# Second MLP product of batches 1 to 7 by seven block products for a pair of token tiles, with memory laid out anew and values cast by their transfer

## The chip, the cores and the metric

The kernel runs on one core of a Trainium2 chip. The metric is the device time of one execution in microseconds (us). The engines are named as the profile names them: PE is TensorE (PEld its weight loads), DVE is VectorE, ACT is ScalarE, POOL is GpSimd and SP is SyncE, which issues transfers and transposes. A trailing q (SPq) is an engine's queue.

## The reference

Attention over 8 batches of 12 heads (448 tokens, 64 features a head), with q and k normalised per token, then a layer norm, a multilayer perceptron of 768 to 3072 to 768 with a relu, and the residual:

```python
q_n, k_n = rmsnorm(q, g_q), rmsnorm(k, g_k)
scores = q_n @ k_n.transpose(0, 1, 3, 2) / sqrt(64)
attn_out = softmax(scores) @ v                      # (8, 12, 448, 64)
x = attn_out.transpose(0, 2, 1, 3).reshape(8, 448, 768)
xn = (x - mean(x)) / sqrt(var(x) + 1e-6) * g_ln
out = x + maximum(xn @ w_ch1, 0.0) @ w_ch2          # 768 x 3072, 3072 x 768
```

All inputs and the output are float32.

## The kernel before

Heads are taken in pairs, six to a batch. A *unit* is one or, in the steady part, two pairs whose q, k and v are loaded and prepared together. Preparation is a list of one-letter pieces (prep_ops): `a` squares the keys on ACT into the tile khl, `c` squares the queries into qn (line L116), `d` and `e` sum the squares on DVE (ssq, L266), `g` turns sums into scales, `i` multiplies keys by the product of both gains on POOL (L274), `j` and `k` split a key into a high and a low fp16 half (khl; L108, L282), `l` and `m` make the fp16 queries (qn; L91, L319), `v` and `w` cast values to fp16 on POOL (v16, vl; L322, L328), `x` transposes the keys into kU and `y` the queries into qU by transfers of SP (L298 to L311). khl, qn and the load tile qkv have two buffers each; kU and qU have two as well.

Attention of a pair runs in seven *steps*: per step one score product (psS, L408) on PE, an exp on ACT (E, L440) and one value product of the pair before (oA, oB; L477, L479). Two PSUM banks named psS and the bank of tr take turns for scores. At a pair's end DVE divides (L490 to L497), writes the tokens' rows x (xl for the last 64 tokens of two batches, put together as a fourth tile), and takes statistics (L990).

Batch 0 is done in phases by token tiles, in an order written out by hand (the table ORDER). For batches 1 to 7 the MLP of batch b runs beside the attention of batch b + 1. mlp_chunks(b) yields *chunks*, each with a cost: 24 up chunks (six matmuls psH, L1056, and a relu on ACT into hT, L1058), and then, for every token tile and half of the 768 output columns, four down chunks of six matmuls of 384 columns (psC, L1090), the result of which DVE scales and adds to x (L1097). Odd batches have four tiles of 128 tokens (up products of 512 columns), even ones three (384 columns). run_rest emits the attention steps between chunks in proportion to cost, so that they end 13 chunks early:

```python
emit()
done += cost
upto(int(min(goal, start + (goal - start) * done / (total - 960 * tail))))   # tail = 13
if self.pos >= goal and items is None:
    items = self.ln_list(b + 1)
```

In those last 13 chunks the layer norm of batch b + 1 runs: the aggregate (L1005), the norm xn of each tile (L1010, on DVE), and its transpose into xnT by SP (L1038). The first up product of batch b + 1 needs all of xnT. Batch 7 has no attention beside it.

psH, psC and a few others share the three PSUM banks of the pool ps_m. PE, ACT, POOL and SP issue in the order of the code; the place of an instruction on DVE is chosen by a scheduler when the program is built, and is then fixed too.

## Time and profile before

| | |
|---|---|
| median of 3 runs | 592.93 us (591.63 to 593.49) |
| the profiled execution | 591.01 us, span 589.4 us |
| PE busy | 577.6 us, 98% of the span |
| ACT, DVE, POOL busy | 353.0, 291.7, 189.5 us |
| second products psC (L1090) | 1368 matmuls |
| up products psH (L1056) | 1008 matmuls |
| DMA | 75.25 MB, 128 GB/s over the span |

The span goes from the first to the last instruction; the execution's own time includes some 1.6 us around it. The busy time of an engine is the sum over its instructions without overlaps; matmuls are pipelined, so the mean of one (323 ns for psC) is longer than the interval between two.

### The profile page before, as it was taken

The numbers are of one execution on the slowest core, as the hardware profiler recorded it, in microseconds if no ns is written. First come the engines' busy times: TensorE is split into PE (matmuls) and PEld (weight loads), VectorE is DVE, ScalarE is ACT, GpSimd is POOL, SyncE is SP. The second block draws the span as 40 slices with busy tenths as digits, with TensorE's granted clock in tenths as the row PEclk, the third lists the DMA queues.
The fourth block names the chain that finished last, engine by engine and source line by source line (L and its number), as shares of the span: only waits on it lengthen the run. The fifth ranks groups of instructions, "written<-read, shape, count | busy, mean of one in ns | idle before, by whom it ended". The sixth has DMA issues, their size and how long they took to land.

```text
span 589.4 us, 12424 instructions
## 1 busy us (share of the span) xinstructions
PE 577.6 (98%) x4971; PEld 360.4 (61%) x4971; DVE 291.7 (49%) x636; ACT 353.0 (60%) x666; POOL 189.5 (32%) x258
## 2 busy tenths in 40 slices
PE   5899999999999999999999999999999999999997
PEld 5799976545666666545566666655566566654565
DVE  6999688345545456624446256815266222540011
ACT  5999773488752997178842797358844477124300
POOL 4648261065350665044350465342502000000000
PEclk9999999999999999999999999999999999999999
DMA  8999998573594987843779596844823220030011
GB/s 266 226 246 219 228 220 213 115 192 89 114 181 125 132 161 115 191 131 66 124 133 158 99 140 140 174 133 92 155 59 88 69 63 1 33 103 1 1 53 57
DMA packets 130321, 75.25 MB, mean 128 GB/s; under 512 B 96564, under 2 KB 120452, under 8 KB 130260
## 3 DMA queue, kind: packets, MB, share of 16 engines
q1 hardware_dynamic: 113712, 44.94, 37.3%
q0 software_dynamic: 16224, 29.27, 23.7%
q8 instruction: 40, 0.66, 0.5%
q10 hardware_dynamic: 324, 0.21, 0.1%
q14 instruction: 21, 0.17, 0.1%
HBM read 52.30 MB, written 11.01 MB: 107 GB/s over the span
## 4 chain that ended last, share of the span: by engine, by line
PE 95%; SPq 2%; DVE 1%; DMA 1%; ACT 0%; issue 0%
PE psC L1090 37%; PE psH L1056 33%; PE psS L408 8%; PE oA L477 5%; PE psU L749 4%; PE oB L479 2%; PE psS L426 2%; PE psS L693 1%; SPq L167 1%; SPq L175 1%; PE oA L725 1%; DMA qkv<-in_q_dram 1%; PE tr L345 1%; PE tr L362 0%; ACT E L704 0%; DVE khl L573 0%
## 5 line engine op out<-in xcount | busy, mean ns | idle before, releaser
L1090 PE MATMUL psC<-w,hT 128*128 128x384 f16 (+1 forms) x1368 | 235.6, 323 | 0.0
L1056 PE MATMUL psH<-xnT,w 128*128 128x512 f16 (+1 forms) x1008 | 217.3, 356 | 0.0
L440 ACT ACTIVATE E<-psS,rr_all 128x448 f16<-128x448 f32 x264 | 164.6, 636 | 58.3 <-PE psS L408 57.6
L1090 PEld LDWEIGHTS <-hT 128*128 128x128 f16 x1368 | 128.2, 98 | 75.9 <-issue 0.4
L1058 ACT ACTIVATE hT<-psH 128x512 f16<-128x512 f32 (+1 forms) x168 | 93.7, 558 | 112.3 <-PE psH L1056 110.8
L1056 PEld LDWEIGHTS <-w 128*128 128x128 f16 x1008 | 91.1, 98 | 77.0 <-issue 2.1
L408 PE MATMUL psS<-qU,kU 128*128 128x448 f16 x252 | 86.3, 352 | 0.0
L477 PEld LDWEIGHTS <-E 128*128 128x128 f16 x792 | 53.6, 98 | 34.4 <-issue 2.1
L1097 DVE SCALAR_TENSOR_TENSOR x<-psC,rs_all,x 128x384 f32<-128x384 f32 x48 | 29.0, 616 | 75.6 <-PE psC L1090 75.1
L274 POOL TENSOR_TENSOR qkv<-qkv,gprod 128x896 f32<-128x896 f32 x19 | 39.5, 2079 | 76.9 <-ACT khl L116 62.4
L477 PE MATMUL oA<-v,E 128*128 128x65 f16 x756 | 57.8, 193 | 0.1
L490 DVE RECIPROCAL rec_all<-oA 128x6 f32<-128x6 f32 x42 | 8.2, 195 | 88.6 <-PE oA L477 88.2
L167 POOL DMA_DIRECT2D qkv<-in_k_dram x14 | 11.1, 796 | 118.3 <-ACT E L440 53.4
L266 DVE TENSOR_REDUCE ssq<-khl 128x14 f32<-128x896 f32 x21 | 22.7, 1083 | 53.3 <-ACT khl L116 53.2
L479 PE MATMUL oB<-v,E 128*128 128x65 f16 x252 | 45.0, 193 | 0.1
L408 PEld LDWEIGHTS <-kU 128*128 128x128 f16 x252 | 24.3, 98 | 15.3
L266 DVE TENSOR_REDUCE ssq<-qn 128x14 f32<-128x896 f32 x21 | 22.8, 1084 | 21.1 <-ACT qn L116 21.1
L91 DVE SCALAR_TENSOR_TENSOR qn<-qkv,rr_all 128x256 f16<-128x256 f32 (+2 forms) x71 | 25.3, 416 | 15.1 <-ACT rr_all L270 15.1
L749 PE MATMUL psU<-xnT,w 128*128 128x128 f16 x432 | 27.0, 219 | 0.0
L749 PEld LDWEIGHTS <-w 128*128 128x128 f16 x432 | 25.2, 98 | 1.5 <-issue 0.4
L479 PEld LDWEIGHTS <-E 128*128 128x128 f16 x264 | 25.4, 96 | 0.3 <-DVE xl L497 0.2
L492 DVE TENSOR_TENSOR x<-oA,rec_all 128x384 f32<-128x384 f32 x42 | 23.4, 558 | 1.3
(161 smaller groups left out, 602.5 us busy)
## 6 DMA issues: line engine op xcount, KB each, us to landing
out_dram<-x SPq DMA_DIRECT2D x20, 384.0 KB, 2.6
qkv<-in_v_dram POOLq DMA_DIRECT2D x15, 384.0 KB, 6.6
qkv<-in_k_dram POOLq DMA_DIRECT2D x14, 384.0 KB, 4.0
qkv<-in_q_dram POOLq DMA_DIRECT2D x14, 384.0 KB, 4.9
w<-in_moe_w_ch_dram POOLq DMA_DIRECT2D x3, 1536.0 KB, 13.2
w<-in_moe_w_ch_dram POOLq DMA_DIRECT2D x8, 576.0 KB, 13.0
qkv<-in_q_dram SPq DMA_DIRECT2D x7, 384.0 KB, 8.0
qkv<-in_v_dram SPq DMA_DIRECT2D x6, 384.0 KB, 10.8
```

The costliest lines, as they stand in the source:

```text
L91: nc.vector.scalar_tensor_tensor(out=out, in0=x, scalar=8.0, in1=r.unsqueeze(2).broadcast_to([x.shape[0], g, D]), op0=ALU.mult, op1=ALU.mult)
L266: nc.vector.tensor_reduce(out=c["ssq"][:, n], in_=c["sq", n], axis=AX.X, op=ALU.add)
L274: _on(nc, f"i{u}", "P").tensor_tensor(out=self.loads[u][1], in0=self.loads[u][1], in1=sh.gprod.unsqueeze(1).broadcast_to([128, g, D]), op= ...
L408: self.nc.tensor.matmul(ps[:, 0:S], c["main"][:, ts(i, 128)], c["q"][:, ts(i // 3, S)], start=True, stop=True)
L440: self.nc.scalar.activation(out=o, in_=c.pop(("ps", i))[:, 0:S], func=AFT.Exp, scale=self.units[u][3][:, g:g + 1], bias=EXP_BIAS)
L477: nc.tensor.matmul(oA[:, t, cs], E[:, ts(t, 128)], rhs, start=(i == 0 and t == 0), stop=(i == 6 and t == 2))
L479: nc.tensor.matmul(oB[:, cs], E[:, 320:448], rhs, start=(i == 0), stop=(i == 6))
L749: nc.tensor.matmul(ps[:, ts(f, 128)], sh.w1[:, dc, ts(4 * k + f, 128)], self.xnT[:, dc, ts(t, 128)], start=(f == 0 and dc == 0), stop=(f = ...
L1056: nc.tensor.matmul(ps[:, 0:N], sh.w1[:, dc, ts(f, 128)], xnT[:, dc, 0:N], start=(dc == 0), stop=(dc == NDC - 1))
L1058: nc.scalar.activation(out=hT[:, f, 0:N], in_=ps[:, 0:N], func=AFT.Relu)
L1090: nc.tensor.matmul(self.psC[:, 0:g[1]], self.hT[:, f, ts(t, 128)], sh.w2[:, h, f, c:c + g[1]], start=(f == 0), stop=(f == NFF - 1))
L1097: self.nc.vector.scalar_tensor_tensor(out=x, in0=self.sums.pop((b, t, g[0]))[:, 0:g[1]], scalar=self.rs[:, b, t:t + 1], in1=x, op0=ALU.mul ...
```

## The change

For two neighbouring token tiles of one batch the second product is a 2 x 2 block product: two row blocks (the tiles a and a + 1) of two inner halves (the first 12 and the last 12 of the 24 chunks of hT, `lo` and `hi`) by two inner halves of two column halves of w2. It is now computed by seven products of blocks with 12 matmuls each, not eight, which needs sums of blocks beforehand and of results behind. In an odd batch two pairs of tiles are done so, in an even batch one pair, and its third tile as before in chunks named U, V and W. Batch 0 keeps the old way.

```diff
+        for f in range(NFF):
+            yield 6 * N / 2.4, (lambda f=f: (up(f), self.after_up(b, f)))
+        yield from self.products(b, n)
+
+    def after_up(self, b, f):
+        if b == 1 and f % 4 == 3:
+            self.weight_sums(f // 4)
+        if f in (11, 17):
+            self.sums_of(0, "3", slice(0, 6) if f == 11 else slice(6, 12), self.xn)
+        if f in (19, 23):
+            self.sums_of(0, "1", slice(0, 6) if f == 19 else slice(6, 12))
...
+    def sums_of(self, a, which, f, room=None):
...
+        if which == "3":
...
+            tt(out=o[:, f], in0=lo(a), in1=lo(a + 1), op=ALU.subtract)
+        elif which == "1":
+            tt(out=lo(a + 1), in0=lo(a + 1), in1=hi(a + 1), op=ALU.add)
+        elif which == "2":
+            tt(out=lo(a), in0=lo(a + 1), in1=lo(a), op=ALU.subtract)
+        else:
+            tt(out=hi(a), in0=hi(a), in1=lo(a), op=ALU.subtract)
...
+        def gather(p6, p7, a):
+            def call():
+                u = kept(a)
+                tt(out=u, in0=six(c[p6][:, 0:384]), in1=u, op=ALU.add)
+                self.free(c.pop(p6))
+                x = six(tiles[a][:, 384:DM])
+                stt(out=x, in0=u, scalar=self.rs[:, b, a:a + 1], in1=x, op0=ALU.mult, op1=ALU.add)
+                tt(out=u, in0=six(c[p7][:, 0:384]), in1=u, op=ALU.add)
+                self.free(c.pop(p7))
...
+            product(key(1), lo(a), wl(0), True, True, sums(a, "2"), keep(key(1), a), read(key(1), a, L))
+            product(key(7), third, wx(1), True, True)
+            product(key(6), lo(a), wx(0), True, True, gather(key(6), key(7), a))
+            product(key(2), hi(a), wh(0), True, True, sums(a, "4"), read(key(2), a, L), *behind,
+                    *([put(a, L)] if end else []))
+            product(key(5), lo(a + 1), wl(1), True, True, read(key(5), a, R, last=False), read(key(5), a + 1, R))
+            product(key(4), hi(a + 1), wx(2), True, True, read(key(4), a + 1, L), put(a + 1))
...
+                product(key(3), hi(a), wh(1), True, True, read(key(3), a, R), put(a, R if end else slice(0, DM)),
+                        *([flush] if a + 2 == n else []))
```

The four sums of a pair are single fp16 tensor_tensor instructions on DVE (L1150 to L1156), those of the first pair of a batch partly in halves after up chunks. Batch 1 also makes three sums of blocks of w2, once for all batches (weight_sums, 24 instructions). A result that is needed twice is kept on ACT (keep, L1209). The bank of each product is freed by its read (L1186, L1194) or by the gather (L1214 to L1223).

Room for the weight sums is found by a new layout. One tile `room` holds load tiles, E rows and weight sums in turn. From unit 9 (STEADY) there is one buffer for khl, one for qn, and one load tile for q and k; E has nine rows handed out one by one; xn has two buffers for batches 2 to 7 instead of four; the sums' scratch rt is single. The three banks of ps_m are handed out by a list written into the code. The values of units from 9 on are loaded straight into v16 and vl as fp16, by six transfers a unit issued by POOL, in place of a load and POOL's casts:

```diff
+        if u >= STEADY and n == 2:
+            s0 = UNIT_PAIR[u] % 6
+            out = self.v16[:, s0:s0 + m].rearrange("p s h j d -> p (s h) j d")
+            for h in range(2 * m):
+                self.nc.gpsimd.dma_start(out[:, h, :, 0:D], self.v[b, hs + h, 0:384].rearrange(
+                    "(p j) d -> p j d", j=3))
+            left = self.v[b, hs:hs + 2 * m, 384:448].rearrange("(w e) p d -> e p w d", e=2)
+            for e in range(2):
+                self.nc.gpsimd.dma_start(self.vl[64 * e:64 * e + 64, s0:s0 + m, e, 0:D], left[e])
+            return
...
-            c["khl"] = self.p_n.tile([128, 14, 2, D], FP16, tag="khl", name="khl")[:, 0:g]
+            c["khl"] = self.split_tile("khl", u >= STEADY)[:, 0:g]
...
-                c["qn"] = self.p_n.tile([128, 14, 2, D], FP16, tag="qn", name="qn")[:, 0:g]
+                c["qn"] = self.split_tile("qn", u >= STEADY)[:, 0:g]
...
+            s = 7 * (UNIT_PAIR[u] - 2)
+            for at, names in ((-6, "V"), (-8, "bai"), (-7, "d"), (-5, "jc"), (-4, "e"), (-3, "kg"), (-2, "lK"),
+                              (-1, "mQ"), (0, "x"), (1, "y")):
```

The last lines set at which attention step, relative to s, each piece of a unit is issued; a unit has 14 steps. K and Q stand for the loads of the next unit's keys and queries, V for the casting load of this unit's values.

The order on DVE at the end of batch 1 is shown next. BN_AGGR is the aggregate and xn the norms of batch 2; psC reads belong to batch 1. Before:

```order
L492 TENSOR_TENSOR x<-oA,rec_all 128x3x128
L497 TENSOR_TENSOR xl<-oB,rec_all 64x128
L990 BN_STATS stat<-x 128x6 x3
L1005 BN_AGGR stat<-stat 128x2 x3
L1010 SCALAR_TENSOR_TENSOR xn<-x,stat,gln 128x768 x3
L1097 SCALAR_TENSOR_TENSOR x<-psC,rs_all,x 128x384 x2
L282 TENSOR_TENSOR khl<-qkv,khl 128x14x64
```

After, at the same place:

```order
L546 TENSOR_TENSOR x<-oA,rec_all 128x3x128
L551 TENSOR_TENSOR xl<-oB,rec_all 64x128
L1045 BN_STATS stat<-x 128x6 x3
L1060 BN_AGGR stat<-stat 128x2 x3
L1065 SCALAR_TENSOR_TENSOR xn<-x,stat,gln 128x768 x2
L1154 TENSOR_TENSOR hT<-hT 128x12x128
L1186 SCALAR_TENSOR_TENSOR x<-psC,rs_all,x 128x384
L308 TENSOR_REDUCE ssq<-khl 128x14
L1065 SCALAR_TENSOR_TENSOR xn<-x,stat,gln 128x768
L1214 TENSOR_TENSOR hT<-psC,hT 128x6x64
```

The second sum of the second pair (L1154) and a read now stand behind two of the three norms, and the third norm behind them.

At the end of batch 2, on DVE, three norms and a fourth for xl stood ahead of the reads; before:

```order
L1005 BN_AGGR stat<-stat 128x2 x4
L1010 SCALAR_TENSOR_TENSOR xn<-x,stat,gln 128x768 x3
L1010 SCALAR_TENSOR_TENSOR xn<-xl,stat,gln 128x768
L1097 SCALAR_TENSOR_TENSOR x<-psC,rs_all,x 128x384 x2
L282 TENSOR_TENSOR khl<-qkv,khl 128x14x64
```

After:

```order
L1060 BN_AGGR stat<-stat 128x2 x4
L1065 SCALAR_TENSOR_TENSOR xn<-x,stat,gln 128x768 x2
L1186 SCALAR_TENSOR_TENSOR x<-psC,rs_all,x 128x384 x3
L1065 SCALAR_TENSOR_TENSOR xn<-x,stat,gln 128x768
L1065 SCALAR_TENSOR_TENSOR xn<-xl,stat,gln 128x768
L1186 SCALAR_TENSOR_TENSOR x<-psC,rs_all,x 128x384
L1194 SCALAR_TENSOR_TENSOR x<-psC,rs_all,x 128x768
```

Three reads (products 5, 5 and 4) have moved between the norms.

On ACT, in batch 2, around the squares of keys and queries (L116), with what each instruction waits for (DMAHW are the transposes and loads of SP, DMASW the loads of POOL); before:

```order
L116 ACTIVATE khl<-qkv 128x896 [waits DMAHW4_49,DMAHW5_49,DMASW7_49,DMAHW6_49,DMASW6_49,DMASW0_49]
L440 ACTIVATE E<-psS,rr_all 128x448 [waits PE_49]
L1058 ACTIVATE hT<-psH 128x384 [waits PE_49]
L440 ACTIVATE E<-psS,rr_all 128x448 [waits PE_49]
L116 ACTIVATE qn<-qkv 128x896 [waits DMAHW1_49,DMAHW2_49,DMAHW0_49,DMAHW3_49,DMASW3_49,DMAHW7_49,DMASW2_49,DMASW1_49]
L440 ACTIVATE E<-psS_5190,rr_all 128x448 [waits PE_49]
```

After:

```order
L116 ACTIVATE khl<-room 128x896 [waits DMAHW5_49,DMAHW6_49,DMASW7_49,DMAHW7_49,DMASW1_49,DMASW0_49]
L1113 ACTIVATE hT<-psH 128x384 [waits PE_49]
L492 ACTIVATE room<-psS,rr_all 128x448 [waits PE_49]
L1113 ACTIVATE hT<-psH 128x384 [waits PE_49]
L492 ACTIVATE room<-psS_5147,rr_all 128x448 [waits PE_49]
L1113 ACTIVATE hT<-psH 128x384 [waits PE_49]
L108 ACTIVATE khl<-room 128x14x64 [waits DVE_49,Pool_49]
L116 ACTIVATE qn<-room 128x896 [waits DMAHW1_49,DMAHW2_49,DMAHW0_49,DMAHW3_49,DMASW4_49,DMAHW4_49,DMASW3_49,DMASW2_49]
L492 ACTIVATE room<-psS,rr_all 128x448 [waits PE_49]
```

Before, the transposes that the squares wait for are those of two units back (the tiles have two buffers); now they are those of the unit just before, and the query square stands one piece later, right behind the key's high half.

## The prediction

> **What bounds the kernel now.** I read the page first (engine shares, chain, costliest groups), then the chain in order of time, a table by stage, VectorE's timeline at the two kinds of batch boundary, and SyncE's queue in one even batch.

> ```profile
> span 589.4 us, 12424 instructions
> PE 577.6 (98%) x4971; PEld 360.4 (61%) x4971; DVE 291.7 (49%) x636; ACT 353.0 (60%) x666; POOL 189.5 (32%) x258
> PE 95%; SPq 2%; DVE 1%; DMA 1%; ACT 0%; issue 0%
> L1090 PE MATMUL psC<-w,hT 128*128 128x384 f16 (+1 forms) x1368 | 235.6, 323 | 0.0
> ```

> TensorE is busy 98% of the span and is 95% of the chain, so each matmul removed is time removed, unless a new wait appears on PE. PE has nowhere to hide one: its idle time is 11.8 us in all. VectorE is half idle on average.

> ```profile
> 175.01 12.68 PE psC L1090 x78
> ...
> 236.03 12.67 PE psC L1090 x78
> ...
> 554.03 31.27 PE psC L1090 x216
> ```

> These are stretches of bare second products: the last 13 chunks of batches 1 and 2, and batch 7's product. 12.68/78 gives 0.1626 us for a matmul of 384 columns; a chunk of six is 0.975 us. (The group's mean of 323 ns counts a pipeline's overlap and is not the price.)

> ```profile
> core 0: us, PE busy (x) PEld busy (x) DVE busy (x) ACT busy (x) POOL busy (x), PEclk, DMA share, GB/s
> 187.70:236.00 48.30, 48.30 (x427) 30.27 (x426) 24.35 (x58) 40.56 (x79) 27.03 (x37) 1.00 0.82 131
> 248.70:312.50 63.80, 63.80 (x477) 34.99 (x475) 25.15 (x59) 45.25 (x81) 27.77 (x38) 1.00 0.61 112
> 554.00:585.30 31.30, 31.29 (x217) 20.23 (x214) 4.74 (x8) 0.60 (x1) 0.00 (x0) 1.00 0.13 47
> ```

> The rows are batch 2 up to its last 13 chunks, batch 3 the same, and batch 7's product. The even batch is the tight one: in 48.3 us ACT works 40.6 (84%) and the DMA engines 82%; the odd batch has 71% and 61%.

> **The saving.** Eleven pairs of token tiles (two in batches 1, 3, 5, 7, one in 2, 4, 6) go from 96 to 84 matmuls each: 132 fewer, 132 x 0.1626 = **-21.5 us**. The third tile of an even batch keeps its 48.

> **New VectorE work.** Its nearest rows:

> ```profile
> L1097 DVE SCALAR_TENSOR_TENSOR x<-psC,rs_all,x 128x384 f32<-128x384 f32 x48 | 29.0, 616 | 75.6 <-PE psC L1090 75.1
> L492 DVE TENSOR_TENSOR x<-oA,rec_all 128x384 f32<-128x384 f32 x42 | 23.4, 558 | 1.3
> L1010 DVE SCALAR_TENSOR_TENSOR xn<-x,stat,gln 128x768 f16<-128x768 f32 x24 | 22.8, 994 | 0.1
> L282 DVE TENSOR_TENSOR khl<-qkv,khl 128x896 f16<-128x896 f32 x20 | 21.6, 1080 | 1.3 <-ACT khl L108 1.3
> L785 DVE COPY xnT<-tr 128x768 f16<-128x768 f16 x2 | 1.1, 548 | 0.0
> L352 DVE COPY kU<-tr 128x960 f16<-128x960 f16 x8 | 5.3, 657 | 0.3 <-PE tr L345 0.2
> ```

> A pair needs four fp16 sums of 128x1536 (sums_of), a gather and six reads instead of four. No row shows a tensor_tensor with fp16 alone. Lower bound: the fp16 copies grow by (657-548)/192 = 0.57 ns a column, so 548 + 768 x 0.57 = 0.98 us. Upper bound: the tensor_tensor rows grow by (1080-558)/512 = 1.02 ns, so 1080 + 640 x 1.02 = 1.73 us. I take 0.98, since the copies share the operand type, and price 1.73 as a rival. A gather is 558 + 616 + 558 + about 1.0 (768 columns, L1010) = 2.7 us. Sums 44 x 0.98 = 43, gathers 11 x 2.7 = 30, extra reads 22 x 0.62 = 14, the 24 weight sums of batch 1 (1536 halved, 0.55 each) 13: about 100 us more, 392 of some 570. Between boundaries that lies beside PE: the odd window would hold 25 + some 16 of 60 us. So it costs nothing there; were the cover gone, PE would wait for a bank of psM.

> [...]

> **Odd boundaries (end of batches 1, 3, 5).** When the last attention ends, VectorE has the next batch's layer norm to do and, new, the pair's second sum.

> ```profile
> 177.14 0.41 DVE L1005 BATCH_NORM_AGGREGATE stat<-stat 128x2 f32<-128x18 f32 x3
> 177.47 2.81 DVE L1010 SCALAR_TENSOR_TENSOR xn<-x,stat,gln 128x768 f16<-128x768 f32 x3
> 180.31 1.14 DVE L1097 SCALAR_TENSOR_TENSOR x<-psC,rs_all,x 128x384 f32<-128x384 f32 x2
> L1038 SPq DMA_TRANSPOSE xnT<-xn x3: 1211/1237/1237, 178.4 to 181.1; - x3
> DMA to landing us min/median/max: 2.8/2.9/2.9
> ```

> In the new order two norms stand ahead of that sum (L1154), so it starts at 177.47 + 2 x 0.94 = 179.35 and ends at 180.33. PE has by then only the second chunk of product 1 and the two of product 7: 175.01 + 3 x 0.975 = 177.94. Product 6 multiplies by the sum (lo(a), overwritten by it), so PE stands 2.4 us. Three times: **+7.2**. The third norm moves behind a read and a reduction, to about 182 to 183; its transpose on SP is late next: 1.2 to issue and 2.9 to land (the last two rows) make 187, and PE's first up product moves by the same 2.4 us from 187.7 to 190. Pair two's product 1 also wants a bank that the reads of product 5 free; VectorE needs about 15 us up to there and PE 15.2, a wait of 0 to 1.3, taken as 0.3, three times: **+0.9**.

> **Even boundaries (end of batches 2, 4, 6).**

> ```profile
> 238.91 2.81 DVE L1010 SCALAR_TENSOR_TENSOR xn<-x,stat,gln 128x768 f16<-128x768 f32 x3
> 241.64 1.01 DVE L1010 SCALAR_TENSOR_TENSOR xn<-xl,stat,gln 128x768 f16<-128x768 f32 x1
> 242.68 0.62 DVE L1097 SCALAR_TENSOR_TENSOR x<-psC,rs_all,x 128x384 f32<-128x384 f32 x1
> ```

> Products 5 (its second chunk), 4 and 3 take 5 chunks, to 236.03 + 4.88 = 240.9, and fill the three banks. Product U then needs the bank of product 5, which two reads free behind two norms: 238.91 + 1.88 + 2 x 0.62 = 242.0. That is 1.05 us, three times: **+3.1** (to 4.5).

> **Batch 1's start.** Five weight sums (5 x 0.55 = 2.75 us) stand ahead of the first batch's norm.

> ```profile
> 98.02 0.20 DVE L490 RECIPROCAL rec_all<-oA 128x6 f32<-128x6 f32 x1 [1.56 <-PE oA L477]
> ```

> The idle 1.56 us takes most: 0 to 1.2, plus a late weight transfer; I take **+0.8**.

> **The single key and query buffers.** From unit 9 khl and qn have one buffer. The squares into them (L116 on ACT) therefore wait for the previous unit's transposes on SP, and in ACT's one row the exps and relus stand behind.

> ```profile
> 196.30 2.39 SPq L298 DMA_TRANSPOSE kU<-khl  x1
> 198.74 2.55 SPq L301 DMA_TRANSPOSE kU<-khl  x2
> 201.38 4.27 SPq L308 DMA_TRANSPOSE qU<-qn  x3
> 205.70 2.94 SPq L311 DMA_TRANSPOSE qU<-qn  x2
> L311 SPq DMA_TRANSPOSE qU<-qn x2: 1241/1446/1652, 205.7 to 207.4; - x2
> DMA to landing us min/median/max: 4.5/4.5/4.5
> L116 ACT ACTIVATE qn<-qkv 128x896 f32<-128x896 f32 x19 | 18.2, 956 | 0.0
> L440 ACT ACTIVATE E<-psS,rr_all 128x448 f16<-128x448 f32 x264 | 164.6, 636 | 58.3 <-PE psS L408 57.6
> ```

> Issued over T = 196.30 to 208.64, they have read their source at T + 12.3 at the earliest; the last, issued at 207.4, landed 4.5 us on, at T + 15.6. A step of an even batch will be about 1.10 us ((48.3-1.95)/42), and the square of the next queries stands nine steps after the first transpose, at T + 9.9: ACT stops for 2.4 to 5.7 us. With three score banks the exp behind it is due for the score three steps on, T + 13.2; square and exp take 1.6, so PE waits 0.7 to 4.0 per block, or nothing where ACT had run ahead. In odd batches the step is 1.43 us, the square due at T + 12.8, and I count nothing: PE's next score is three long steps off. Four blocks lie in batches 2 and 4 (batch 6 has no such successor). I take 1.2 each, nearer the low end because the exps themselves now wait 57.6 us for PE's scores (last row), so ACT has some lead: **+4.8**, ends 0 and 16.

> **Other edits together.** V of later units comes by casting transfers on POOL some twenty steps before its use; it removes POOL's casts and adds six issues per unit on an engine 32% busy: nothing. The E rows, two xn buffers and the explicit banks make no wait of PE by the order, except those named. ACT's eleven keeps (384 columns each, under the exp's 636 ns for 448) hide in the window's idle sixth. In batch 7 no attention or norm stands on VectorE, and 8 sums, 2 gathers and 13 reads make about 21 of 27 us. The tail behind PE's end stays.

> **Sum.** -21.5 + 7.2 + 0.9 + 3.1 + 0.8 + 4.8 = -4.7 us. The profiled run took 591.01 us (span 589.4), so 586.3 by it; the median of the runs is 592.93, 1.9 more, so I forecast **588.3**. Without the ACT term it is 583.5, with its upper end 599.5.

> **Rivals.**
> *The transposes win (slower).* The DMA engines decide in even batches.

> ```profile
> q1 hardware_dynamic: 9530, 2.46, 42.8%
> q0 software_dynamic: 1434, 3.80, 39.4%
> ```

> In 188 to 236, q1 moved 258-byte packets in 0.428 x 48 x 16/9530 = 34.5 ns each, 7.5 bytes a ns; q0 moved 2650-byte ones in 211 ns, 12.6 a ns. V is a third of q0, 2.1 us of all engines per unit. Cast, it is 1792 pieces of 64 values; at 34.5 ns 3.9 us. Three units add 5.3 us: 39.6 + 5.3 = 44.9 of 46.3 us, 97%. Then transposes land later, both squares block, and score matmuls themselves may wait for kU and qU. The forecast gain is gone once the four blocks cost 2.4 us each instead of 1.2; up to there (593) it ends as no change; at 3.2 each it is 588.3 + 8.0 = 596.3, and with a DMA bound of 1 us more in each even batch 599. Against it: in the window above PE is busy 48.30 of 48.30 us, so no transpose is late today, and the odd batches have room. [...]

> *Sums at 1.73 us (slower).* Odd boundaries +0.75 each and 2.4 more for banks, even ones and batch 7 a few: +10 to 13, so 598 to 601. The page's idle half of VectorE speaks against saturation, not against the boundary waits.

> *All but the boundary waits hidden (faster still).* No ACT term, half the bank waits: 580 to 583.5.

> *The clock drops (no change).*

> ```profile
> 3.75 1.46 PE L879 MATMUL psW<-id 128*128 128x128 f16 x12 [3.75 <-POOL id masks.py:199]
> 13.93 1.28 PE L879 MATMUL psW<-id 128*128 128x128 f16 x20
> ```

> After idling PE ran at half rate (122 ns against 64), and the later granted clock is 1.00 in every window. PE had worked from 11.6 almost without a gap before it was at full rate at 13.9; half of 2.3 us, after three stalls of 2.4 us, is 3.5: 591.8. [...]

> **How the numbers follow.** Forecast 0.42 (own range 584 to 593), transposes win 0.21, slow sums 0.08, all hidden 0.17, clock 0.06, some other wait (K and Q loads into one buffer, issued 8 steps ahead) 0.06, mostly slower. A measurement tells about 0.3% (1.8 us) from no change. Faster by more (under 591.1): 0.37 of the forecast and the hidden case, 0.54. Same: 0.05 of the forecast, the clock's 0.06, and 0.07 of the transposes' mild cases, 0.18. Slower (over 594.7): the rest of those, 0.28. The range, 580 to 599, leaves out about one in ten on each side.

> **What would show it.** Second-product matmuls of 1224 in all, not 1368 (144 of them batch 0's; the last tile's halves are split finer before); PE waits of about 2.4 us for L1154 at three odd boundaries, about 1 us for L1186 at the even ones; ACT waiting at L116 for transposes in batches 2 and 4, with PE waiting for L492 behind it; L1150 to L1156 near 0.98 us; DVE busy near 390. The prediction fails if PE's waits outside the boundaries exceed 10 us, if the sums take 1.7 us, or if kU and qU appear as what PE waits for.

## The result, and the profile after

The changed kernel takes 647.08 us (median of 4 runs, 642.49 to 650.47), the kernel before 592.59 us (4 runs, 591.63 to 593.49): ratio 1.0915, 95% interval 1.0844 to 1.0985. The forecast was 588.3 us, and its range ended at 599. The profiled execution took 646.58 us.

From the page of the changed kernel, the lines that answer to those shown of before:

```profile
span 645.0 us, 12430 instructions
PE 577.5 (90%) x4827; PEld 352.9 (55%) x4827; DVE 390.3 (61%) x791; ACT 354.9 (55%) x677; POOL 212.6 (33%) x269
PEclk9999999799987999999999899999998899999999
PE 19%; DVE 5%; ACT 1%; DMA 1%; issue 0%; DVEq 0%
```

There are 144 matmuls fewer (4971 before, 4827 now: the 132 of the saving, and 12 of the last tile, whose halves were split before). Yet PE is busy as long as before, 577.5 us against 577.6. Its idle time went from 11.8 to 67.5 us, and the clock row shows slices below 9, which the row of before has nowhere. So two things are to be explained: 55.7 us of new idle time, and some 21 us by which the remaining matmuls became slower.

PE's waits in the changed kernel (in all, times, longest):

```profile
PE oA L529 <- DVE x L546: 13.7, 6, 4.1
PE psC L1176 <- DVE hT L1218: 9.4, 4, 3.6
PE psC L1176 <- DVE hT L1154: 7.0, 3, 2.3
PE psH L1111 <- DVE x L1296: 7.0, 1, 7.0
PE psS L479 <- ACT room L492: 6.7, 13, 0.9
PE psS L450 <- ACT room L492: 4.7, 2, 2.5
PE psC L1176 <- DVE x L1186: 4.4, 3, 1.9
```

These seven rows add up to 52.9 us, nearly all of the 55.7: VectorE 41.5, ACT 11.4. L1154 was forecast nearly to the tenth (7.2), and L1186 (3.1 to 4.5) within its ends. Two have no counterpart in the forecast: L546, the division at a pair's end, and L1218, the second half of a gather.

**L546.** VectorE's timeline in batch 1, beside the first pair's products, and PE's stop:

```profile
176.20 1.01 DVE L1194 SCALAR_TENSOR_TENSOR x<-xnT,rs_all,x 128x768 f32<-128x768 f32 x1
...
177.33 0.95 DVE L1156 TENSOR_TENSOR hT<-hT 128x1536 f16<-128x1536 f16 x1
178.20 0.61 DVE L1186 SCALAR_TENSOR_TENSOR x<-psC,rs_all,x 128x384 f32<-128x384 f32 x1
178.72 0.95 DVE L1150 TENSOR_TENSOR hT<-hT 128x1536 f16<-128x1536 f16 x1
...
179.89 0.95 DVE L1152 TENSOR_TENSOR hT<-hT 128x1536 f16<-128x1536 f16 x1
180.76 0.18 DVE L544 RECIPROCAL rec_all<-oA 128x6 f32<-128x6 f32 x1
181.18 0.56 DVE L546 TENSOR_TENSOR x<-oA,rec_all 128x384 f32<-128x384 f32 x1
181.79 0.27 PE L529 MATMUL oA<-v,room 128*128 128x65 f16 x3 [3.81 <-DVE x L546]
```

PE's queue stands from 177.98 with a value product that needs the bank oA; the division that frees it stands on VectorE behind three sums, a read and a piece of the preparation, with no gap between them. VectorE is 61% busy over the span and full over the 13 us ahead of that division. In batches 3 and 5 the same stop takes 4.13 us each.

**Batch 1's start.** VectorE's timeline there, and PE's stop:

```profile
119.54 0.56 DVE L1139 TENSOR_TENSOR room<-w,room 128x768 f16<-128x768 f16 x1 [6.51 <-DMA qU<-room]
122.09 0.56 DVE L1139 TENSOR_TENSOR room<-w,room 128x768 f16<-128x768 f16 x1 [1.99 <-DMA qU<-room]
122.57 0.61 DVE L1296 SCALAR_TENSOR_TENSOR x<-psC,rs_all,x 128x384 f32<-128x384 f32 x1
123.23 4.86 PE L1111 MATMUL psH<-xnT,w 128*128 128x512 f16 x12 [6.98 <-DVE x L1296]
```

The third weight sum writes a part of `room` that still holds queries being transposed. VectorE stops twice for the transposes; the read of batch 0's last product (L1296) stands behind, the bank it frees comes late, and PE stops for 6.98 us. The 12 matmuls that follow take 4.86 us.

**The clock.** That last row leads to the slower matmuls. From 80 us on, the granted clock of this trace changes only at the edges of a fixed grid of 3.413 us. Of the experiments below, "Also ACT relieved" shows 1.00 in the stretches from 112.25 to 522.98 us and a fall to 0.50 at 584.6 us, where PE is done; "The same ACT edits with the old eight products" shows 1.00 from 111.49 us to the end. Some cells of that grid in the changed kernel (PE busy, weight loads, VectorE, ACT, POOL, then the granted clock, DMA share, GB/s):

```profile
192.39:195.80 3.41, 1.17 (x8) 0.49 (x5) 3.41 (x8) 0.80 (x3) 3.41 (x5) 1.00 0.49 40
195.80:199.21 3.41, 3.32 (x11) 1.60 (x12) 1.98 (x4) 0.00 (x0) 1.28 (x3) 0.50 1.41 143
199.21:202.63 3.42, 1.39 (x9) 0.61 (x8) 3.31 (x6) 0.00 (x0) 0.00 (x0) 1.00 0.37 100
202.63:206.04 3.41, 3.41 (x13) 1.67 (x11) 1.38 (x3) 0.00 (x0) 0.00 (x0) 0.50 0.18 73
345.99:349.40 3.41, 1.45 (x9) 0.68 (x7) 3.41 (x9) 0.80 (x3) 3.41 (x5) 1.00 0.35 23
349.40:352.81 3.41, 2.12 (x12) 1.09 (x12) 2.06 (x4) 0.00 (x0) 1.56 (x3) 1.00 1.49 155
```

The rows come in pairs, a cell and the next. Where PE worked 1.17 or 1.39 us of a cell, the next one is granted half the clock; where it worked 1.45, the next is whole. The pairs at 192.39 and 345.99 are the same stop of 2.34 us for L1154 in batches 1 and 3: in the one all but 0.1 us of it lies within a cell, in the other it lies across an edge. In this trace, from 80 us on, every cell at full clock with 2.03 us of idle time or more was followed by a cell at half clock, and none with 1.96 us or less. Half-clock cells of the changed kernel add up to 30.7 us; without some 3.1 us in which PE stood idle in them, PE did in 27.6 us what it does in 13.8.

Where the other 7 to 8 us of slower matmuls come from was not separated.

### The profile page after: what moved, and what is told of

Read it like the earlier page. It is cut to its first block, busy times and chain, and to the rows that moved or that the text cites. A ratio compares the mean times of both kernels' runs of the same rounds, so it can differ in the third digit from the quotient of the medians.

```text
span 645.0 us, 12430 instructions
## 1 busy us (share of the span) xinstructions
PE 577.5 (90%) x4827; PEld 352.9 (55%) x4827; DVE 390.3 (61%) x791; ACT 354.9 (55%) x677; POOL 212.6 (33%) x269
## 5 line engine op out<-in xcount | busy, mean ns | idle before, releaser
L492 ACT ACTIVATE room<-psS,rr_all 128x448 f16<-128x448 f32 x264 | 162.9, 633 | 62.6 <-PE psS L450 62.0
L1176 PEld LDWEIGHTS <-hT 128*128 128x128 f16 x996 | 96.6, 101 | 85.8 <-issue 14.4
L1111 PEld LDWEIGHTS <-w 128*128 128x128 f16 x1008 | 92.1, 98 | 85.8 <-issue 11.4
L1176 PE MATMUL psC<-w,hT 128*128 128x384 f16 (+1 forms) x684 | 123.1, 329 | 13.8 <-DVE hT L1218 9.4
L316 POOL TENSOR_TENSOR room<-room,gprod 128x896 f32<-128x896 f32 x19 | 39.6, 2083 | 166.4 <-ACT khl L116 166.3
L529 PEld LDWEIGHTS <-room 128*128 128x128 f16 x792 | 53.7, 99 | 53.5 <-DVE x L546 16.0
L529 PE MATMUL oA<-v,room 128*128 128x65 f16 x756 | 59.3, 195 | 13.7 <-DVE x L546 13.7
L1176 PE MATMUL psC<-room,hT 128*128 128x384 f16 x312 | 62.9, 352 | 7.0 <-DVE hT L1154 7.0
L1186 DVE SCALAR_TENSOR_TENSOR x<-psC,rs_all,x 128x384 f32<-128x384 f32 (+1 forms) x65 | 38.7, 608 | 24.1 <-PE psC L1176 23.6
L259 POOL DMA_DIRECT2D v<-in_v_dram x64 | 49.8, 781 | 0.0
L531 PE MATMUL oB<-v,room 128*128 128x65 f16 x252 | 45.7, 195 | 0.2
L203 POOL DMA_DIRECT2D room<-in_k_dram x15 | 12.3, 817 | 69.2 <-DVE khl L324 69.2
L531 PEld LDWEIGHTS <-room 128*128 128x128 f16 x264 | 25.7, 97 | 1.0 <-DVE xl L551 0.7
## 6 DMA issues: line engine op xcount, KB each, us to landing
w<-in_moe_w_ch_dram POOLq DMA_DIRECT2D x3, 1536.0 KB, 13.3
```

The source lines that it names most:

```text
L259: self.nc.gpsimd.dma_start(out[:, h, :, 0:D], self.v[b, hs + h, 0:384].rearrange("(p j) d -> p j d", j=3))
L316: _on(nc, f"i{u}", "P").tensor_tensor(out=self.loads[u][1], in0=self.loads[u][1], in1=sh.gprod.unsqueeze(1).broadcast_to([128, g, D]), op= ...
L492: self.nc.scalar.activation(out=o, in_=c.pop(("ps", i))[:, 0:S], func=AFT.Exp, scale=self.units[u][3][:, g:g + 1], bias=EXP_BIAS)
L529: nc.tensor.matmul(oA[:, t, cs], E[:, ts(t, 128)], rhs, start=(i == 0 and t == 0), stop=(i == 6 and t == 2))
L531: nc.tensor.matmul(oB[:, cs], E[:, 320:448], rhs, start=(i == 0), stop=(i == 6))
L1111: nc.tensor.matmul(ps[:, 0:N], sh.w1[:, dc, ts(f, 128)], xnT[:, dc, 0:N], start=(dc == 0), stop=(dc == NDC - 1))
```

## The experiments

Two theories went into them. **Q**: VectorE's one row of instructions. It does each new thing in order, and what PE needs (the division, a sum, a read) stands behind what PE doesn't need yet. **M**: the memory laid out anew (single key and query buffers, two xn buffers, E rows) makes ACT and the transposes late, whatever the products.

**The new layout with the old eight products.**

```diff
-            yield 6 * N / 2.4, (lambda f=f: (up(f), self.after_up(b, f)))
-        yield from self.products(b, n)
+            yield 6 * N / 2.4, (lambda f=f: up(f))
...
+        for t, g in order:
+            for s in range(4):
+                yield 6 * g[1] / 2.4, (lambda t=t, g=g, s=s: down8(t, g, s))
```

> The changed kernel with the old second product (eight block products, no sums, no gathers); all of the new memory layout, the single buffers, the casting transfers of V and the new steps of preparation stay. Theory Q (the time is lost in VectorE's one queue, where sums, gathers, reads and the attention's divisions wait for each other and PE for them): the waits for L1154, L1218, L546 and L1296 are gone, only ACT's blocks at L116 in batches 2 and 4 remain, some 2 to 4.6 us each, so 595 to 602. Rival M (the layout loses it: single buffers and V's small transfers keep the DMA engines full): PE waits stay in every batch, 620 or more.

Measured: 604.87 us (603.67 to 606.52) beside 592.33 of before, ratio 1.0207 (1.0182 to 1.0232). PE's share and the waits that before hasn't:

```profile
PE 582.8 (96%) x4971; PEld 361.7 (60%) x4971; DVE 292.6 (48%) x636; ACT 353.4 (58%) x666; POOL 212.7 (35%) x269
PE psH L1111 <- DMA xnT<-xn: 4.7, 2, 3.0
PE psS L479 <- ACT room L492: 3.2, 8, 0.5
```

The layout alone costs 12.5 us of the 54.5, a little more than Q's upper end. Part of it lies at a place that the forecast set at nothing: with two xn buffers the up phase waits for the last transpose (3.01 us at the end of batch 2, 1.66 at the end of batch 4). So M is a part, and the products add 42 us though they save 21.5. The changed kernel itself has no stop of PE on xnT in its list; there VectorE alone waits for transposes that still read xn (8.1 us).

**Without the sums of hidden blocks.** The 44 sums (L1150 to L1156) are left out.

```diff
-        tt = self.nc.vector.tensor_tensor
+        tt = lambda **kw: None
```

> The changed kernel with the 44 sums of hidden blocks (L1150 to L1156) left out, so that the products take unsummed blocks; weight sums, gathers, reads and the layout stay. Q: the three waits of 2.3 us for L1154 vanish, the three of about 4 us for the division behind L1150/L1152/L1156 shrink by some 3 us each, the ones for the gather stay near 2; with about four half-rate windows fewer (1.7 each) 647 - 7 - 9 - 7 = 624. M: nothing but the 7 us of L1154 goes, about 640.

Measured: 633.89 us (2 runs, 633.62 and 634.17), ratio 1.0704 (1.0675 to 1.0732).

```profile
PE psC L1176 <- DVE hT L1218: 16.5, 4, 5.0
PE oA L529 <- DVE x L546: 3.0, 4, 1.0
```

This kernel leaves out the sums, so its output is not the reference's; it serves for its times only. The stops on L1154 are gone and those on L546 fell from 13.7 to 3.0 us, which shows that the sums ahead of the division make most of them. But PE then comes earlier to L1218 and waits 7.1 us more there: 17.7 us of stops went, and the time fell by 13.2. The time lay between what the two theories gave.

**The third weight sums later in the code.**

```diff
+        if b == 1 and f in (15, 19, 23):
+            for k in range((f - 15) // 2, (f - 15) // 2 + 2):
+                self.third_sum(k)
...
-        tt(out=wt[:, 2, f], in0=b21, in1=wt[:, 0, f], op=ALU.subtract)
```

> The changed kernel with the third weight sum of batch 1 (L1139) issued after up chunks 15, 19 and 23 instead of from chunk 3 on; same work. Q: L1139 writes the part of room from which SP still transposes queries, VectorE stops for 8.5 us there and the read behind it frees a bank late; moved, the 7.0 us wait of PE at 116 and the 6.8 us at half rate behind it (2.1 us of work) go: 647 - 9 = 638. If that wait is batch 0's last bank by itself, or the half rate has another cause, 645 to 647.

Measured: 643.59 us (640.44 and 646.74). A miss, and an edit that didn't do what it was meant to: VectorE's order is chosen when the program is built, and the sums were again put early (125.0 to 133.9 us, where up chunk 15 is only at 153.6), with 7.8 us of waiting for the queries' transposes as before (8.5). Two stops took the place of the one:

```profile
PE psS L479 <- ACT room L492: 12.7, 12, 7.4
PE tr L384 <- DVE qU L409: 4.9, 2, 4.7
```

The 7.4 us come behind the third sums; the 4.7 us lie earlier, behind another weight sum that VectorE now did while its weights were still on their way.

**Stops of set length in the kernel before.** Instructions on VectorE that rewrite xnT in place, in batch 7's up phase, so that PE stops there.

```diff
+            for _ in range({4: 3, 9: 4, 14: 6, 19: 8}.get(f, 0) if b == B - 1 else 0):
+                nc.vector.scalar_tensor_tensor(out=xnT[:, 0, 0:256], in0=xnT[:, 0, 0:256], scalar=1.0,
+                                               in1=xnT[:, 0, 0:256], op0=ALU.mult, op1=ALU.max)
```

> The kernel before, with VectorE operations in place on xnT between up chunks 3/4, 8/9, 13/14 and 18/19 of batch 7 (3, 4, 6 and 8 of about 0.42 us each, which leave xnT as it is), so that PE stands about 1.4, 1.8, 2.7 and 3.5 us with nothing else in the batch. Theory C (stops of about 2 us already bring the half clock): half rate behind the last three, each some 3.4 us long and 1.7 us of work: 592.6 + 9.4 + 5 = 607. Rival (only a stop as long as a whole window of 3.4 us does): half rate behind the last one at most, 602 to 604.

Measured: 602.80 us (one run), with stops of 0.36, 0.82, 1.74 and 2.66 us. The last two, with the 30 matmuls behind each:

```profile
548.08 6.65 PE L1059 MATMUL psH<-xnT,w 128*128 128x512 f16 x30 [1.74 <-DVE xnT L1055]
557.39 8.34 PE L1059 MATMUL psH<-xnT,w 128*128 128x512 f16 x30 [2.66 <-DVE xnT L1055]
```

8.34 less 6.65 is 1.69 us, half of a cell of 3.41: the 2.66 us stop cost 4.35. The clock's drop needs no other part of the change. The time alone would fit the rival that was written down with it: the stops came out shorter than meant (1.4 to 3.5 us), and the clock dropped behind the last one only. What speaks against that rival is that this stop is shorter than a cell.

**The kept sum out of hT.** The first result of a second pair is kept in 384 fp32 columns laid over hT's tiles (columns 128 to 256 of chunks 12 to 17), while product 2 reads columns 256 to 384 of the same chunks. They share no element, but the product waits for L1218 all the same. Here it is kept in free E rows.

```diff
-            return self.hT[:, nf:nf + 6, 128:256].bitcast(FP32)
+            if not rows:
+                rows.extend(sorted(self.free_rows[:2]))
+            i, j = rows
+            return self.room[:, 448 * i:448 * i + 896 * (j - i)].rearrange(
+                "p (k s) -> p k s", k=2)[:, :, 0:384].bitcast(FP32)
```

> The changed kernel with the kept result of a batch's second pair (kept(2)) in two free E rows of room instead of hT; no work added or left out, VectorE's order by the scheduler as before. Theory Q with a false dependence (the fp32 view of kept(2) in hT is taken to overlap the block hi(2), so product 2 waits for L1218, which writes kept(2), though no element is shared): PE's stops before that product (2.0, 3.6, 1.9 and 1.9 us) go, and some two half-rate windows with them: 647 - 9.4 - 3.4 = 634. Rival (product 2 waits for a bank, which the gather frees): nothing moves, 645 to 648.

Measured: 637.54 us (635.47 and 639.61), ratio 1.0741 (1.0641 to 1.0842). The wait for L1218 is gone from the list, the rest stands nearly as it was (L546 13.9, L1154 7.0, L1186 4.3, and 7.0 for L1296, which is L1303 here). So the bank that the gather frees was not what product 2 waited for; the wait hung on where the sum is kept, though no element is shared. That the build draws a dependence between the two strided views is the reading of it. It was worth 9.5 us by the medians, with intervals that leave some us open.

**VectorE's order by hand.** The same products and the same preparation steps. VectorE issues in code order; weight sums go singly and later (after up chunks 4 to 19), some sums in halves, a gather in parts; the norms and their transposes have places of their own; the kept sum is out of hT. These go together: but for the kept sum, none was tried by itself. Three of the 20 lines that say what follows which down chunk in an odd batch (s sums, k keep, r read, g parts of the gather, p and fl stores; .0 and .2 the pair):

```diff
-        with tc.manual_schedule(engines=manual):
+        with tc.manual_schedule(engines=manual | {ENG.DVE}):
...
+1: s2.0 k.0 r1.0
+5: g1.0 g2.0
+6: g3.0 g4.0
...
-        if b == 1 and f % 4 == 3:
-            self.weight_sums(f // 4)
+        if b == 1:
+            for x in range(24):
+                if WK[x] == f:
+                    self.weight_sum(x)
```

> The same sums, products and layout as the changed kernel, with VectorE's instructions issued in an order written by hand: weight sums one by one after up chunks 4 to 19, the second pair's sums in halves between the products of the first, its second sum ahead of the norms, gathers in four parts, and kept(2) outside hT. The steps of preparation stay. Theory Q: of PE's 52 us of stops only ACT's remain (about 10 us in batches 2 and 4, 3 in batch 1) and half a us here and there, and with no stop above 2.3 us the clock stays: 590.7 - 21.5 + some 25 to 35 = 595 to 606. Rival M (the layout and its transfers): 625 or more, since the layout is as it was.

Measured: 616.43 us (614.49 and 618.38), ratio 1.0386 (1.0289 to 1.0483): 30.6 us less than the change, 10 more than the upper end expected. What remains on PE and, last, on VectorE:

```profile
PE psS L539 <- ACT room L552: 6.5, 12, 0.9
PE oA L589 <- DVE x L606: 5.6, 5, 2.5
PE psH L1173 <- ACT hT L1175: 3.7, 2, 2.1
DVE ssq L368 <- ACT qn L173: 35.4, 12, 5.7
```

VectorE now waits 35.4 us for ACT's squares of the queries (5.0 in the changed kernel). In a row by hand, everything behind such a reduction is late too. That the clock stays where no stop exceeds 2.3 us was the author's estimate: in the changed kernel a stop of 2.03 us (from 199.63 us) was followed by a half-clock cell, and one of 2.48 us (from 388.85) by none.

**Also ACT relieved.** In addition the key's high half (j) of units from 9 on runs on POOL, the pieces stand at other steps, and the attention ends 15 chunks early, not 13.

```diff
-            for at, names in ((-6, "V"), (-8, "bai"), (-7, "d"), (-5, "jc"), (-4, "e"), (-3, "kg"), (-2, "lK"),
-                              (-1, "mQ"), (0, "x"), (1, "y")):
+            for at, names in ((-7, "ba"), (-6, "Vd"), (-5, "i"), (-4, "j"), (-3, "c"), (-2, "ke"), (-1, "gK"), (0, "lQx"), (1, "my")):
...
-        tail = 13
+        tail = 15
```

> fixdve with three more edits: the copy of a key's high half (j, 0.94 us on ACT) of units 9 on goes to POOL, the pieces of preparation stand at other steps (a -7, j -4, c -3, e and k -2, g -1, l 0, m and y 1), and attention ends 15 chunks before a batch's end instead of 13. Theory Q with ACT as the second engine that is full: ACT's stops of PE go too, and most of the 21.5 us of matmuls come out: 580 to 588, faster than before. Rival (the single buffers bind, wherever the pieces stand): 592 or more.

Measured: 590.21 us (10 runs, 588.44 to 595.28) beside 592.03 of before (19 runs, 590.81 to 598.42), ratio 0.9957 (0.992 to 0.9994). It beats the changed kernel by 57 us, and the kernel before by an amount at the edge of what can be told; the expectation was missed by 2 us.

```profile
span 587.4 us, 12451 instructions
PE 562.0 (96%) x4827; PEld 347.0 (59%) x4827; DVE 393.9 (67%) x806; ACT 341.7 (58%) x661; POOL 229.5 (39%) x285
PE psC L1239 <- DVE hT L1217: 3.0, 7, 0.7
PE psS L539 <- ACT room L552: 2.8, 5, 1.2
DVE ssq L368 <- ACT qn L173: 8.9, 9, 2.2
112.25:251.19 138.94, 133.90 (x1023) 77.09 (x1021) 105.29 (x215) 84.74 (x164) 68.61 (x84) 1.00 0.74 124
522.98:587.40 64.42, 58.80 (x327) 31.25 (x326) 23.52 (x46) 15.31 (x26) 0.00 (x0) 0.98 0.12 43
```

VectorE is busier than in the changed kernel (393.9 us, 67%), and PE waits for it far less: no stop in its list beyond batch 0 is longer than 1.3 us. So it was not the amount of that work, but its order, the false wait and what ACT held up. The last two rows are batches 1 and 2 together, and batch 7.

**The same ACT edits with the old eight products.**

```diff
-ENGINE = dict(x.split(":") for x in """ j1:P C1:A QC0.0:A QC0.2:A qG2.0:V qm2.0:P qm2.4:P
+ENGINE = dict(x.split(":") for x in """ j9:P j10:P ... j31:P j1:P C1:A QC0.0:A QC0.2:A qG2.0:V qm2.0:P qm2.4:P
```

(units 9 to 31), and the steps as above, on the new layout with the old products.

> The kernel layout (new memory, old second product) with the copies j on POOL and the pieces at the steps of best1; attention ends 13 chunks early as before. If layout's 12.5 us are ACT's blocks and late transposes, most of them go: 592 to 597. If the casting transfers and single buffers cost by themselves, it stays at 602 to 605. Against best1 it also tells what the seven products are worth when nothing stops them: theory Q says 10 to 14 us.

Measured: 594.87 us (10 runs, 593.66 to 596.04), ratio 1.003 (1.000 to 1.006), as expected. Its span, and the stretches that answer to the two of the kernel ahead:

```profile
span 592.0 us, 12550 instructions
PE 580.1 (98%) x4971; PEld 361.6 (61%) x4971; DVE 293.3 (50%) x636; ACT 340.4 (58%) x650; POOL 226.6 (38%) x285
111.49:250.10 138.61, 138.13 (x1060) 80.53 (x1057) 67.45 (x153) 84.69 (x161) 67.57 (x84) 1.00 0.80 130
525.15:592.00 66.85, 62.73 (x364) 34.45 (x361) 6.53 (x15) 14.33 (x24) 0.00 (x0) 1.00 0.09 30
```

Ten of the layout's 12.5 us go with one copy moved off ACT and pieces set apart. Against this kernel, on nearly equal ground (here the attention ends 13 chunks early, not 15, and the scheduler orders VectorE), the seven products are worth 594.87 - 590.21 = 4.7 us of 21.5. The expectation had 10 to 14, so that part of it was missed. PE's busy time falls by 18.1 us, its idle time rises by 13.5 (11.9 to 25.4). In batches 1 and 2, PE does 4.2 us less and takes 0.3 us more; in batch 7, where no attention runs beside, 2.4 us come out.

**The ACT edits alone, on the changed kernel.** j on POOL and the steps; VectorE's order as the scheduler put it.

> The changed kernel with the two edits on ACT and POOL alone: the key's high-half copy of units from 9 on POOL, the preparation pieces at the steps of the best version; the order on VectorE stays as the scheduler put it, with the read behind L1218 and the batch-1 sums as they are. If the ACT edits have a worth of their own wherever they stand, they take the 26 us that they took behind the VectorE edits (616.4 to 590.2), so about 621. If VectorE's queue is the larger cause and the ACT edits take only the stops on L492 (2.2 and 2.5 us with their half-clock stretches, and a dozen of 0.5 to 0.9), about 10 to 17 us as between the two layout kernels, so 630 to 637, with the stops on L546, L1154 and L1218 of 2 to 4 us and the one of 7 us at batch 1's start still there.

Measured: 633.77 us (633.65 to 634.39), ratio 1.0713 (1.0695 to 1.0731).

```profile
PE oA L529 <- DVE x L546: 9.4, 4, 3.3
PE psC L1175 <- DVE hT L1217: 7.6, 4, 1.9
PE psC L1175 <- DVE hT L1153: 7.0, 3, 2.3
PE psH L1110 <- DVE x L1295: 6.9, 1, 6.9
PE psS L479 <- ACT room L492: 2.3, 6, 0.5
```

The stops on ACT fall from 11.4 to 2.3 us. Those on VectorE mostly stay: 37.0 us (with 6.1 for the reads, L1185) where they were 41.5. The time lies where the second reading had it, 630 to 637. With the other kernels this makes a square:

| | VectorE by the scheduler | VectorE by hand, kept sum out of hT |
|---|---|---|
| ACT as in the change | 647.1 | 616.4 |
| ACT relieved | 633.8 | 590.2 |

The ACT edits are worth 13.3 us alone and 26.2 us behind the others (with the attention two chunks earlier there). VectorE's side (order, pieces and kept sum) is the larger cause either way, 30.6 or 43.6 us; the kept sum, tried by itself, took 9.5 of that. Some 13 us go only when both sides are mended. The rows fit that: VectorE's wait of 35.4 us for the query squares is 8.9 us in the kernel with both edits. How much of the 13 us that link carries, and how much the two chunks, was not tried by itself.

## Why the prediction was wrong

- **The step that failed**: "Between boundaries that lies beside PE ... So it costs nothing there; were the cover gone, PE would wait for a bank of psM." The total was right (forecast about 392 us of VectorE work, measured 390.3), and the sums, forecast at 0.98 us, take 0.95 (1.06 on L1154). 768 fp16 columns of L1152 take 0.56 us, and 384 fp32 columns of L546 as much. What failed was reasoning from shares: a mean of 61% says nothing of what stands in the row when PE needs one instruction of it. The bank named was the wrong one too: not psM but oA, freed by the division. It cost 13.7 us of stops, more in clock. The prediction's own sign of failing, over 10 us of stops outside the boundaries, was met by that row alone.
- **A wait not seen at all**: L1218, 9.4 us. The forecast asked which elements a product reads, not which instructions the program makes it wait for; the order of the changed program, with its waits, was there to be read before any run.
- **Batch 1's start**, forecast at +0.8, stopped PE for 6.98 us. The forecast counted the weight sums' durations, and not what their output lies over.
- **The clock**, a rival at 0.06, worked out at 3.5 us: about 14 us. The rival took stops of 2.4 us as the question, which was right: of the three for L1154, two were followed by a half-clock cell. It counted three stops, where the trace has fourteen of 1.89 us or more from 80 us on.
- **The layout's xn buffers and E rows**, forecast at nothing: part of the 12.5 us measured for the layout alone, with 4.7 us of stops on xnT there. In the changed kernel PE has no such stop, so what they cost it is not shown.
- **What held**: the matmul counts; the odd boundaries, +7.2 against 7.0 of stops on L1154; the even ones, +3.1 (to 4.5) against 4.4. The +0.9 for the second pair's banks has no row in PE's list. ACT's blocks at L116 stop PE for 4.7 us against 4.8, by the mechanism told, but the sum is luck: two stops of 2.2 and 2.5 us and not four of 1.2. The key squares in batches 3 and 5 wait 2.0 and 1.5 us for kU without stopping PE, as the forecast had it for odd batches. The further 6.7 us in 13 stops on L492 were not in the sum.
- **The main rival** (the transposes win, 0.21) is false as told: no row of the changed kernel's list has PE waiting for a transpose into kU or qU, and the DMA engines are less loaded in batch 2 than before (0.73 against 0.83, over 66.1 and 61.0 us). Transposes held up VectorE and ACT; PE has no row that names one.

On ACT, the first of the two blocks at L116 is this row:

```profile
235.71 0.95 ACT L116 ACTIVATE qn<-room 128x896 f32<-128x896 f32 x1 [2.19 <-DMA qU<-qn]
```

By terms: -21.5 of the saving, +55.7 of idle time and +21.4 of slower matmuls (what is left of PE's busy time) make 55.6 us of span (589.4 to 645.0).

## What to carry to other kernels

An engine half idle on average is no cover by itself (VectorE, 61% busy, stopped PE for 41.5 us here): for each new instruction on it, write down what stands behind it in its row and when the bound engine wants that; cut the new work into pieces and set them behind what is wanted first. When buffers are put over one another, read the waits in the built program: a view laid over another can bring a wait though no element is shared (9.4 us on L1218 here). A saving on the engine that sets the end shrinks by every wait it gains: here an eighth fewer matmuls in the paired products came to 4.7 of 21.5 us after both queues were put in order.
